# The fourth slot of a fused attention and mixture-of-experts kernel uses seven products

## The chip, the cores and the metric

The kernel runs on one core of one Trainium2 chip. A core has a matrix engine, TensorE (PE in the rows, with its weight loads as PEld), a vector engine, VectorE (DVE), a scalar engine, ScalarE (ACT), a general engine, GpSimd (POOL), and SyncE (SP), which here issues transfers. Each engine works through its own queue in order; they meet through semaphores. The metric is the time on the device in microseconds, lower is better.

## What is computed

An attention over a small memory feeds a mixture of experts. Eight batches of 576 tokens make 4608 tokens of 512 values (8 heads of 64):

```
a   = softmax(phi, over the 576 tokens)             # 32 memory slots per head
k_m = a^T k ;  v_m = a^T v                          # per batch and head
x   = softmax(q k_m^T / 8) v_m                      # 4608 x 512, all heads side by side
e   = argmax(x w_gate)                              # one of 8 experts per token
out = gate * sigmoid(x w_output_gate)[e] * (relu(x w1[e]) w2[e])   # 512 -> 1024 -> 512
```

Only the last line, the two layers of the experts, is touched by the change. The matmuls have to be nearly as exact as float32. Each operand is therefore kept as a high and a low part, and a product of two matrices is three matmuls (high by high, low by high, high by low: `PASS`).

## The kernel before

**Stages.** The attention runs batch pair by batch pair and writes the rows of x to a table in DRAM (`xs`). Routing counts the tokens of each expert and writes lists of rows. The experts' work is then done in *slots*: a slot is 576 tokens of one expert. Eight big slots are numbered 0 to 7. Slots 0 to 3 (`NPE`) are filled from the first half of the tokens, so they can start while the attention of the second half still runs; slots 4 to 7 (`NPL`) come from lists that the late routing writes (`route_late`). Slots 0 and 1 share their time with the rest of the attention, slot 2 begins when the late routing ends.

**One slot.** `nine` (L1382) does a slot. Its first layer gives 1024 hidden values per token, in matmuls of 288 columns (half a slot's tokens). It comes in two forms:
- `plain` (L1266, matmuls at L1278): 4 weight pieces x 2 x 2 halves of the tokens x 12 matmuls, used for the slots in `WHOLE`, 0 to 3;
- `seven` (L1285, matmuls at L1306 in `product`): both matrices are cut in two by two, and seven products of sums and differences replace eight products (Strassen's scheme in Winograd's form); each product is 4 x 6 matmuls. Its intermediate results are copied from PSUM into tiles `keep` (L1313) and added on DVE (L1317). Used for the slots in `SEVEN`, 4 to 7.

The second layer (L1409) takes 112 matmuls of 512 columns in either form. Its steps are numbered 16 to 35 after the 16 of the first layer; `finish_y` (L1227) scales its results and scatters them with an indirect transfer of POOL (L1237).

**Preparing the next slot.** This is done within the slot before, mostly in its second layer.
- `gather` (L463, transfers at L468): POOL fetches the 576 rows of the next slot, full rows of 576 floats, into tile `xg`. There is one such buffer.
- For a `plain` slot, `turn_x` (L1045) turns the rows on PE (16 of L1108 with 128 columns, 4 of L1113 with 64), ACT and DVE split the result into high and low parts (L1070, L1071).
- For a `seven` slot, `relay` (L474) copies `xg` in 16 transfers on SP (L484) from SBUF tile to SBUF tile into `xq`, so that DVE's transposes of 32 by 32 blocks (L1074) finish the turn. Then the differences of the parts (L1092), their high parts on ACT (L1086, L1095) and their low parts on DVE (L1097, L1100).
- Weights are loaded by SP (L522), split into high (ACT, L564) and low (DVE, L569). A `seven` slot also needs four sums of weight parts, `S1` to `S4` in `prep` (L526): S3, S1 and S4 on DVE (L538, L544, L546), S2 on POOL (L542).

**Layouts.** The memory is laid out anew as stages end. `settle` (L1481) follows slot 1. `reopen` (L1493) finishes the late routing, closes its pools, opens the pool `st` (which holds `xq`, `keep`, the sums and the parts of differences), and gives weights two more raw buffers, seven in all. `rebank` (L1502) cuts PSUM into two sets of four banks, and is called in a slot whose successor is a `seven` slot. `run` (L1508) walks over the slots and calls `reopen`; its `hook` is called after each step of a slot and issues the gathers, the copies of the relay (from steps `RELAY` = 5 and 8 of the slot before) and the steps of the routing. When a slot's successor is a `seven` slot, `nine` uses tables of its own for the order of the preparation (`TURN6`, `EXTRA6`, `SUMS6` after a `plain` slot, `TURN7`, `EXTRA7`, `SUMS7` after a `seven` slot).

Of the kernel before, what the change touches and what calls it, by code (L numbers as in the profile page):

```python
# [30 lines left out]
NPE, NPL, NSS = 4, 4, 28  # L31
# [31 lines left out]
EXTRA7 = (2, 6, 9, 12, 17, 19)  # L63
GATHER = {8: 2, 12: 2, 16: 1}
LAST = 1
OPEN = 3
WHOLE = tuple(range(NPE))
SEVEN = tuple(range(NPE, NPE + NPL))
PROD = ("P1", "P2", "P6", "P5", "P3", "P7", "P4")
SPLITS = {"P1": (0, 2), "P6": (2,), "P5": (0, 2)}  # L70
SUMS = {"P6": "S2", "P5": "S1", "P3": "S4", "P7": "S3"}
# [9 lines left out]
def attention_moe(tc, phiT, kv, qT, wgo, wall, out):  # L81
# [3 lines left out]
    with contextlib.ExitStack() as ctx:  # L85
# [343 lines left out]
        def force():  # L429
            clock[0] += 1  # L430
            (rou if rou.gens else late if late.gens else att).step()
# [22 lines left out]
        for s in range(NSLOT):  # L454
# [3 lines left out]
            slots.append({"s": s, "big": big, "q0": NCL * j if big else NCL * NPL + j - NPL, "idx": idx[nm],  # L458
                          "rows": 4 * S if s < NPE else NTOK, "nm": nm, "quart": s not in WHOLE, "seven": s in SEVEN,
                          "known": False, "listed": False})  # L460
# [13 lines left out]
        def relay(z, to=4):  # L474

            if not z["quart"]:
                return
            if "xq" not in z:
                z["xq"] = env["st"].tile([P, NCL, 4, P], F32, name="xq")
                z["a"] = 0  # L480
            for a in range(z["a"], to):
                for b in range(4):
                    m = 1 if not z["big"] else NCL if b < 2 else NCL - 1
                    nc.sync.dma_start(z["xq"][32 * a:32 * a + 32, 0:m, b],  # L484
                                      z["xg"][32 * b:32 * b + 32, 0:m, XQ * a:XQ * a + P])
                z["a"] = a + 1
# [109 lines left out]
        def gathers(i, must=0, n=999, to=2):  # L596

            while True:
                if drip.gens:
                    drip.step(999 if gat[0] <= must else n)  # L600
                    if drip.gens:
                        break
                    n = 0
                if gat[0] >= min(gat[1], i + to):
                    break
                z = order[gat[0]]
                if not z["listed"]:
                    if gat[0] >= must:
                        break
                    force()  # L610
                    continue
                if gat[0] >= must and n <= 0:
                    break
                drip.gens.append(gather(z))
                gat[0] += 1
# [589 lines left out]
        def grow(k):  # L1205
            nonlocal mo
            if k == 0:
                mo = ctx.enter_context(tc.tile_pool(name="mo", bufs=1, reuse_waits="tile"))
            for r, n in zip((ring, raw, xgs), GROW[k]):
                if n:  # L1210
                    p = ctx.enter_context(tc.tile_pool(
                        name=f"{r.name}{k + 1}", bufs=n, reuse_waits="tile"))
                    r.add(p, n)
# [267 lines left out]
        def settle():  # L1481

            att.finish()
            pso.close()
            pa.close()
            env["rl"] = prl.enter_context(tc.tile_pool(name="rl", bufs=1, side="right", reuse_waits="tile"))
            env["cap"] = raw.size
            grow(1)
            env["ps"] = prp.enter_context(tc.tile_pool(name="p1", bufs=7 - NPK, space=PSUM, reuse_waits="tile"))
# [3 lines left out]
        def reopen():  # L1493

            late.finish()
            prl.close()
            prt.close()
            env["st"] = ctx.enter_context(tc.tile_pool(name="st", bufs=1, side="right", reuse_waits="tile"))
            grow(2)
            env["cap"] = raw.size  # L1500
# [7 lines left out]
        def run(st):  # L1508

            lo, hi = st.lo, st.hi  # L1510
            while not order[lo]["known"]:
                force()
            st.fetch()
            if lo:
                gat[:] = lo, hi

            def hook(step, new):
                if step < 16 or not drip.gens:
                    gathers(i)
                if i + 1 < hi and order[i + 1]["seven"]:  # L1520
                    if step in RELAY and (gat[0] > i + 2 or gat[0] > i + 1 and not drip.gens):
                        relay(order[i + 1], 2 * RELAY.index(step) + 2)
                clock[0] += not att.gens
                att.step(HOOK[0])
                (rou if rou.gens else late).step(HOOK[1])

            for i in range(lo, hi):
                if i == OPEN:
                    reopen()
                gathers(i, i + 1, 0)  # L1530
                if i == lo:
                    for c in range(4):
                        turn_x(order[i], c)

                def nxt(c):
                    if i + 1 < hi:
                        gathers(i, i + 2)
                        turn_x(order[i + 1], c)

                if order[i]["big"]:  # L1540
                    nine(i, st, nxt, hook)
                else:
                    single(i, st, nxt)
                if "rl" not in env and (i == LAST or not att.gens):
                    settle()
# [5 lines left out]
        env["open"] = True  # L1551
        n = NPE + NPL
        run(stream)
        used = nc.values_load(slot[0:1, NSLOT:], min_val=0, max_val=NSS)  # L1554
        with tc.If(used > 0):
            run(Stream(n, n + 1))
            with tc.If(used > 1):
                run(Stream(n + 1, n + 4))
                with tc.If(used > 4):
                    run(Stream(n + 4, NSLOT))  # L1560
# [44 lines left out]
```

## Time and profile before

| | |
|---|---|
| median of 3 runs | 550.5 us (548.32 to 551.82) |
| profiled execution, its own time | 550.38 us |
| its span in the trace | 548.6 us |
| TensorE (PE) busy | 500.8 us, 91% |
| VectorE (DVE) busy | 362.8 us, 66% |
| ScalarE (ACT) busy | 273.0 us, 50% |
| GpSimd (POOL) busy | 175.0 us, 32% |
| mean over 16 DMA engines | 188 GB/s |

The page of the profile gives busy time per engine, and forty equal slices of the span with a digit for the busy tenths of each engine. The timeline lists instructions in order of their start, with like neighbours merged: start, length, engine, line, operation, what it writes and reads, count; brackets give the idle time before and what ended it. Matmuls overlap in the pipeline, so the length of one (0.29 us) is more than the step from one to the next (0.13 us); steps between starts are what counts.

### The profile page before, as it was taken

What the parts mean: (1) busy time and instruction counts of PE and PEld (TensorE: products, weight loads), DVE (VectorE), ACT (ScalarE), POOL (GpSimd) and SP (SyncE); (2) the same over time, 40 slices, a digit from 0 to 9 for tenths busy, and PEclk for the clock granted to TensorE, in tenths of its full rate; (3) what the DMA queues carried; (4) which work ended last, traced back from release to release, by engine and by line L of the source; (5) the groups of instructions that cost most, each with busy time, mean ns of one, the idle gap of its engine ahead of it and who ended that gap; (6) DMA issues with size and microseconds to landing.
All of it is one profiled execution on the core that took longest, in us unless ns stands there. A gap on an engine that the chain in (4) does not pass through costs nothing. (4 is left out here: it accounts for less than half of the span.)

```text
span 548.6 us, 10934 instructions
## 1 busy us (share of the span) xinstructions
PE 500.8 (91%) x4141; PEld 432.0 (79%) x4141; DVE 362.8 (66%) x802; ACT 273.0 (50%) x526; POOL 175.0 (32%) x202
## 2 busy tenths in 40 slices
PE   3688677759999999999999999999999999999993
PEld 2455445539987899889988998998899899889982
DVE  4387799766971678975424459578779867878500
ACT  4467474254643453243324325576485666648320
POOL 2334465554251233214022315512612350220021
PEclk9969998769999999999999999999999999999998
DMA  8999999976543575317332830891485179130011
GB/s 324 419 375 384 413 374 396 321 279 192 202 128 133 159 271 132 112 42 249 84 118 71 299 84 11 275 245 48 149 260 169 39 235 258 46 106 21 1 49 44
DMA packets 44414, 103.11 MB, mean 188 GB/s; under 512 B 9600, under 2 KB 18880, under 8 KB 43968
## 3 DMA queue, kind: packets, MB, share of 16 engines
q1 hardware_dynamic: 38464, 82.26, 45.3%
q0 software_dynamic: 5888, 20.06, 10.5%
q8 instruction: 34, 0.56, 0.4%
q14 instruction: 28, 0.23, 0.1%
HBM read 77.23 MB, written 20.35 MB: 178 GB/s over the span
## 5 line engine op out<-in xcount | busy, mean ns | idle before, releaser
L1409 PE MATMUL bps<-whl,hh 128*128 128x512 f32 x576 | 173.2, 393 | 0.0
L1409 PEld LDWEIGHTS bps<-whl,hh 128*128 128x128 f32 x576 | 107.5, 188 | 22.6
L569 DVE TENSOR_TENSOR whl<-w,whl 128x1024 fp32r<-128x1024 f32 x72 | 88.1, 1232 | 52.5 <-ACT whl L564 51.9
L1278 PE MATMUL bps<-xh,whl 128*128 128x288 f32 x512 | 105.1, 297 | 0.0
L1409 PE MATMUL bps<-whl,hl 128*128 128x512 f32 x224 | 87.3, 390 | 0.0
L1278 PEld LDWEIGHTS bps<-xh,whl 128*128 128x128 f32 x512 | 83.0, 188 | 1.3 <-issue 0.6
L564 ACT CAST whl<-w 128x1024 fp32r<-128x1024 f32 x72 | 74.6, 1049 | 3.2 <-PE bpc L1409 2.0
L1278 PE MATMUL bps<-xl,whl 128*128 128x288 f32 x256 | 75.5, 295 | 0.0
L1237 POOL DMA_INDIRECT out<-y,idx_oa x20 | 27.3, 1365 | 110.4 <-ACT y L1236 86.9
L1246 ACT ACTIVATE hh<-bps 128x288 fp32r<-128x288 f32 x64 | 26.4, 412 | 57.9 <-PE bps L1278 56.7
L1237 POOL DMA_INDIRECT out<-y,idx_ol x20 | 21.8, 1090 | 101.4 <-ACT y L1236 66.7
L1409 PEld LDWEIGHTS bps<-whl,hl 128*128 128x128 f32 x224 | 42.1, 188 | 8.2
L1278 PEld LDWEIGHTS bps<-xl,whl 128*128 128x128 f32 x256 | 48.3, 189 | 0.1
L1251 DVE SCALAR_TENSOR_TENSOR hl<-bps,hh 128x288 fp32r<-128x288 f32 x64 | 26.9, 421 | 31.7 <-ACT hh L1246 31.6
L1236 ACT ACTIVATE y<-bps,gx 128x512 f32<-128x512 f32 x28 | 19.3, 690 | 49.7 <-PE bps L1409 44.7
L1306 PE MATMUL bpc<-th,whl 128*128 128x288 f32 x192 | 39.7, 295 | 0.0
L1306 PE MATMUL bpc<-xh,whl 128*128 128x288 f32 x192 | 39.7, 295 | 0.0
L892 ACT COPY xo<-bpd 128x576 f32<-128x576 f32 x36 | 22.5, 639 | 25.2 <-PE bpd L890 17.6
L857 POOL TENSOR_TENSOR ea<-ea,mx 128x512 f32<-128x512 f32 (+1 forms) x20 | 19.2, 961 | 43.5 <-DVE mx L855 41.7
L1306 PEld LDWEIGHTS bpc<-xh,whl 128*128 128x128 f32 x192 | 31.3, 188 | 0.2
L1306 PEld LDWEIGHTS bpc<-th,whl 128*128 128x128 f32 x192 | 31.3, 188 | 0.0
L1246 ACT ACTIVATE hh<-keep 128x288 fp32r<-128x288 f32 x48 | 21.1, 446 | 18.8 <-DVE keep L1317 18.8
(263 smaller groups left out, 890.8 us busy)
## 6 DMA issues: line engine op xcount, KB each, us to landing
w<-wall SPq DMA_DIRECT2D x64, 512.0 KB, 5.1
kvt<-kv SPq DMA_DIRECT2D x32, 512.0 KB, 8.2
xs<-xo SPq DMA_DIRECT2D x16, 576.0 KB, 7.0
qt<-qT SPq DMA_DIRECT2D x16, 512.0 KB, 9.1
ph<-phiT SPq DMA_DIRECT2D x3, 1152.0 KB, 11.7
xq<-xg SPq DMA_DIRECT2D x32, 80.0 KB, 4.8
kv<-kv SPq DMA_DIRECT2D x4, 512.0 KB, 9.9
xq<-xg SPq DMA_DIRECT2D x32, 64.0 KB, 3.9
```

What stands on the lines that cost most here:

```text
L564: A.copy(hl[:, 0], w[:])
L569: V.tensor_tensor(hl[:, 1], w[:], hl[:, 0].bitcast(F32), ALU.subtract)
L857: G.tensor_tensor(eav, eav, mx[:, 0:n].unsqueeze(2).to_broadcast([P, n, M]), ALU.subtract)
L892: A.copy(xo[:, c % 2], px[:, :, 0:2 * XQ])
L1236: A.activation(y[0:n], py[0:n], AF.Copy, scale=z["g"][0:n, k:k + 1])
L1237: G.indirect_dma_start(out=out, out_offset=bass.IndirectOffsetOnAxis(ap=z["idx"][1][0:n, z["q0"] + k:z["q0"] + k + 1], axis=0), in_=y[0:n] ...
L1246: A.activation(h_[:, j, c:e], src, AF.Relu)
L1251: V.scalar_tensor_tensor(lo, src[:, s0 - c:s1 - c], 0.0, h_[:, j, s0:s1].bitcast(F32), ALU.max, ALU.subtract)
L1278: T.matmul(pb, w[:, b, o:o + P], x[a][:, cc, c * SL // 2:(c + 1) * SL // 2], start=(n == 0), stop=(n == 11))
L1306: T.matmul(pb, w[:, b, o:o + P], z[x][a][:, kc], start=(first and n == 0), stop=(n == 5), skip_group_check=not first)
L1409: T.matmul(py, a, w[:, b, DM * f:DM * f + DM], start=(u == 4 and f == 0 and n == 0), stop=(u == 7 and f == 1 and n == len(ps) - 1))
```

## The change

Three edits, in the tables at the head of the file and in `run`:
- `WHOLE` becomes slots 0 to 2 and `SEVEN` slots 3 to 7. Slot 3 takes the form `seven` with everything that belongs to it: weights in the other cut, `relay` in place of turns on PE, the four sums, the results kept in tiles.
- `OPEN` becomes `(2, 2)`: `reopen` is called from `hook` after step 2 of slot 2, instead of ahead of slot 3. Buffers of the pool `st` are needed then by slot 2's steps.
- With slot 3 a `seven` slot, slot 2 prepares by the tables `TURN6`, `EXTRA6`, `SUMS6` and calls `rebank`, as slot 3 does in the kernel before, and slot 3 prepares by `TURN7`, `EXTRA7`, `SUMS7`, as slots 4 to 6 do.

```diff
--- before.py
+++ after.py
@@ -63,9 +63,9 @@
 EXTRA7 = (2, 6, 9, 12, 17, 19)
 GATHER = {8: 2, 12: 2, 16: 1}
 LAST = 1
-OPEN = 3
-WHOLE = tuple(range(NPE))
-SEVEN = tuple(range(NPE, NPE + NPL))
+OPEN = (2, 2)
+WHOLE = tuple(range(NPE - 1))
+SEVEN = tuple(range(NPE - 1, NPE + NPL))
 PROD = ("P1", "P2", "P6", "P5", "P3", "P7", "P4")
 SPLITS = {"P1": (0, 2), "P6": (2,), "P5": (0, 2)}
 SUMS = {"P6": "S2", "P5": "S1", "P3": "S4", "P7": "S3"}
@@ -1515,6 +1515,8 @@
                 gat[:] = lo, hi
 
             def hook(step, new):
+                if (i, step) == OPEN:
+                    reopen()
                 if step < 16 or not drip.gens:
                     gathers(i)
                 if i + 1 < hi and order[i + 1]["seven"]:
@@ -1525,8 +1527,6 @@
                 (rou if rou.gens else late).step(HOOK[1])
 
             for i in range(lo, hi):
-                if i == OPEN:
-                    reopen()
                 gathers(i, i + 1, 0)
                 if i == lo:
                     for c in range(4):
```

On PE, in slot 2's second layer (the L1409 rows) and at its end; whl is a weight piece, xg the gathered rows, - is the kernel before, + the changed one:
```order
 L1409 MATMUL bps<-whl,hh 128x512
-L1108 MATMUL bps<-ident,xg 128x128 x4
-L1113 MATMUL bps<-ident,xg 128x64 x4
+L1306 MATMUL bpc<-xh,whl 128x288
+L1306 MATMUL bpc<-xl,whl 128x288
+L1306 MATMUL bpc<-xh,whl 128x288 x2
```
The turns are gone, here the first eight of twenty, and L1409 is followed by the first of the seven products. In the whole program L1108 and L1113 lose 16 and 4 instructions, L1278 loses 192 and L1306 gains 168.

On DVE, from the end of slot 2's first layer on; first the kernel before:
```order
L1251 SCALAR_TENSOR_TENSOR hh<-bps,hh 128x64
L569 TENSOR_TENSOR whl<-w,whl 128x1024
L1234 TENSOR_TENSOR y<-bps,y 64x512
L569 TENSOR_TENSOR whl<-w,whl 128x1024
L1071 TENSOR_TENSOR xl<-bps,xh 128x512
L1071 TENSOR_TENSOR xl<-bps,xh 128x4x64
L1071 TENSOR_TENSOR xl<-bps,xh 128x512 x3
```
and at the same place in the changed kernel (`s_3801` is the tile of S2):
```order
L1251 SCALAR_TENSOR_TENSOR hh<-bps,hh 128x64
L538 TENSOR_TENSOR w<-w 128x1024
L1074 STREAM_TRANSPOSE xg<-xq 128x576 x4
L1234 TENSOR_TENSOR y<-bps,y 64x512
L1092 TENSOR_TENSOR xq<-xg 128x576
L1092 TENSOR_TENSOR xq<-xg,xq 128x576
L1092 TENSOR_TENSOR xq<-xg 128x576
L1092 TENSOR_TENSOR xq<-xg,xq 128x576
L569 TENSOR_TENSOR whl<-s_3801,whl 128x1024
L1097 TENSOR_TENSOR xl<-xg,xh 128x576 x3
L544 TENSOR_TENSOR w<-s_3801,w 128x1024
L1100 TENSOR_TENSOR xl<-xq,xh 128x576
```
The low parts of turned rows give way to the transposes, differences and sums of a seven-product slot; the rows ahead of this place, the late routing's among them, stand as they did.

On POOL, from the gather for slot 3 (`idx_ga`) on; first the kernel before:
```order
L468 DMA xg<-xs,idx_ga 128x576 x4
L468 DMA xg<-xs,idx_ga 64x576
L1237 DMA out<-y,idx_oa 4608x512 x5
L468 DMA xg<-xs,idx_gl 128x576 x4
L468 DMA xg<-xs,idx_gl 64x576
L542 TENSOR_TENSOR s_4306<-w 128x512 x2
```
and the changed kernel:
```order
L468 DMA xg<-xs,idx_ga 128x576 x4
L468 DMA xg<-xs,idx_ga 64x576
L542 TENSOR_TENSOR s_3801<-w 128x512 x2
L1237 DMA out<-y,idx_oa 4608x512 x2
L468 DMA xg<-xs,idx_gl 128x576 x4
L468 DMA xg<-xs,idx_gl 64x576
```
The gather for slot 3 keeps its place, S2 for slot 3 comes behind it, and the gather for slot 4 (`idx_gl`) stands behind two of slot 2's outputs instead of five.

## Rows read from the trace of the kernel before

**Rows 1.** The page: TensorE's busy time, busy tenths and granted clock in 40 slices.
```profile
PE 500.8 (91%) x4141; PEld 432.0 (79%) x4141; DVE 362.8 (66%) x802; ACT 273.0 (50%) x526; POOL 175.0 (32%) x202
...
PE   3688677759999999999999999999999999999993
...
PEclk9969998769999999999999999999999999999998
```

**Rows 2.** Timeline of TensorE at the borders of slots and layers: start, length, instruction, count.
```profile
244.28 0.29 PE L1278 MATMUL bps<-xh,whl 128*128 128x288 f32 x1
...
269.71 1.55 PE L1409 MATMUL bps<-whl,hh 128*128 128x512 f32 x6
...
297.59 0.29 PE L1278 MATMUL bps<-xh,whl 128*128 128x288 f32 x1
...
348.44 0.29 PE L1306 MATMUL bpc<-xh,whl 128*128 128x288 f32 x1
```

**Rows 3.** Busy time by stretch, between the borders of layers, columns in its first line.
```profile
core 0: us, PE busy (x) PEld busy (x) DVE busy (x) ACT busy (x) POOL busy (x), PEclk, DMA share, GB/s
244.28:269.72 25.44, 25.44 (x194) 25.44 (x193) 13.63 (x31) 10.52 (x20) 7.23 (x6) 1.00 0.59 187
269.72:297.59 27.87, 27.87 (x134) 22.93 (x133) 7.74 (x11) 10.36 (x17) 3.94 (x4) 1.00 0.23 71
297.59:323.03 25.44, 25.44 (x194) 25.44 (x193) 13.24 (x28) 10.51 (x20) 7.24 (x6) 1.00 0.68 222
323.03:348.44 25.41, 25.41 (x115) 21.02 (x113) 18.18 (x24) 10.92 (x18) 14.44 (x8) 1.00 0.27 76
348.44:370.83 22.39, 22.39 (x169) 22.39 (x168) 17.25 (x39) 16.25 (x34) 5.68 (x5) 1.00 0.87 255
370.83:396.26 25.43, 25.43 (x114) 21.02 (x113) 21.43 (x28) 13.74 (x21) 11.04 (x9) 1.00 0.31 90
```

**Rows 4.** Timeline of TensorE in slot 2's second layer, at the first turns.
```profile
285.15 0.39 PE L1409 MATMUL bps<-whl,hl 128*128 128x512 f32 x1
285.38 0.39 PE L1409 MATMUL bps<-whl,hh 128*128 128x512 f32 x1
285.61 0.60 PE L1108 MATMUL bps<-ident,xg 128*128 128x128 f32 x4
...
286.53 0.50 PE L1409 MATMUL bps<-whl,hh 128*128 128x512 f32 x1
```

**Rows 5.** Timeline of POOL, SP and DVE in slot 3: preparation of slot 4.
```profile
300.13 1.52 POOL L468 DMA_INDIRECT xg<-xs,idx_gl  x1 [0.30 <-issue]
...
313.75 10.98 SPq L484 DMA_DIRECT2D xq<-xg  x16
...
326.51 2.76 DVE L1074 STREAM_TRANSPOSE xg<-xq 128x576 f32<-128x576 f32 x4 [1.19 <-DMA xq<-xg]
...
333.68 2.09 DVE L1097 TENSOR_TENSOR xl<-xg,xh 128x576 fp32r<-128x576 f32 x3
...
339.50 1.22 DVE L546 TENSOR_TENSOR w<-w,s 128x1024 f32<-128x1024 f32 x1
...
336.55 6.19 POOL L1237 DMA_INDIRECT out<-y,idx_oa  x1 [4.44 <-ACT y L1236]
```

**Rows 6.** Timeline of POOL, SP and DVE at the start of slot 2.
```profile
247.24 1.10 POOL L468 DMA_INDIRECT xg<-xs,idx_ga  x1 [0.31 <-issue]
...
252.57 1.68 POOL L468 DMA_INDIRECT xg<-xs,idx_ga  x1 [0.30 <-issue]
...
253.47 0.33 SPq L522 DMA_DIRECT2D w<-wall  x1
...
244.74 0.21 DVE L264 SCALAR_TENSOR_TENSOR idx_ol<-iv,i 128x48 int32<-128x48 f32 x1
```

**Rows 7.** Timeline at the end: TensorE's last matmul and the last output.
```profile
539.52 0.39 PE L1409 MATMUL bpc<-whl,hh 128*128 128x512 f32 x1
...
541.33 0.98 POOL L1237 DMA_INDIRECT out<-y,idx_ol  x1 [4.87 <-ACT y L1236]
```

## The prediction

> **What bounds the kernel now.** I read the page first: TensorE (PE) is busy for 91% of the span, and in its forty slices PE is at 9 from the tenth slice to the last but one, with the granted clock at 9 or more there, which is the 2.4 GHz level [rows 1]. So the question is not which engine is busiest, but whether PE ever waits in the stretch that the change touches. I then cut the span at the borders of the slots, read from the timeline of PE (a slot's first layer begins with L1278 or L1306, its second with L1409) [rows 2], and asked for the busy time of each engine between those borders [rows 3]. There PE is busy for the whole of every stretch: 25.44 of 25.44, 27.87 of 27.87 us and so on, at clock 1.00. No engine has to become faster for this stretch to become shorter; instructions have to leave PE.
>
> The same table gives the price of each layer directly, as lengths:
> - first layer without products saved (slots 2 and 3): 25.44 us each;
> - first layer of seven products (slots 4 and 5): 22.39 and 22.40 us;
> - second layer with the next slot's twenty PE turns in it (slot 2): 27.87 us;
> - second layer before a seven-product slot, so without turns: 25.41 us (slot 3) and 25.43 us (slot 4).
>
> **The change part by part.**
> *Fewer matmuls.* Slot 3's first layer has 4 x 2 x 2 x 12 = 192 matmuls now and will have 7 x 4 x 6 = 168. By the lengths that is 25.44 - 22.39 = 3.05 us (24 matmuls at 25.44/192 = 0.1325 us are 3.18 us; the seven-product layer runs at 22.39/168 = 0.1333 us). Slot 3's second layer goes from 25.41 to 25.43 us, since it now prepares slot 4 from a seven-product slot: +0.02. Together -3.03 us.
>
> *Turns leave PE.* Sixteen L1108 and four L1113 instructions go from slot 2's second layer. By the lengths, 27.87 - 25.41 = 2.46 us. The timeline agrees for the first eight of them: from the matmul at 285.38 to the next one at 286.53 are 1.15 us, of which one matmul's own step is 0.23 (285.15 to 285.38), so 0.92 us for eight [rows 4]; the remainder, 1.54 us, leaves 0.51 us for each of the three groups of four that follow.
>
> The Trainium skill's page "TensorE: Matmul & The Clock Gate", section "Back-to-back issue gap", gives N/2.4 + 2.5 ns for a warm matmul of N columns: 122.5 ns for 288 columns and about 56 ns for a turn of 128. By it the 24 matmuls would be 2.94 us and the twenty turns an estimated 1.1 us, 4.1 us in all and 546.3 us for the kernel. This case's lengths are larger for both (132.5 ns a matmul, 2.46 us for the turns), and the sum goes by the lengths.
>
> *What takes their place, and what hides it.* The preparation that slot 3 now makes for slot 4 will be made once more, in slot 2 for slot 3: gather into xg, sixteen copies from SBUF tile to SBUF tile on SP (L484), then S3, four transposes, four differences, the low parts and the sums on VectorE (DVE), S2 on GpSimd (POOL). The trace shows this very sequence in slot 3 [rows 5]: gather issued from 300.13, copies from 313.75 for 10.98 us, transposes at 326.51, the operands of the first product finished at 333.68 + 2.09 = 335.77, the last sum of weights at 339.50 + 1.22 = 340.72. Slot 4 begins at 348.44 [rows 2]. So the first operands have 12.7 us of slack and the last item of the list 7.7 us, and PE does not wait. I take 7.7 as the slack, the smaller.
>
> In slot 2 it starts at nearly the same phase: the gather for slot 3 is already there, issued from 247.24, 2.96 us into the slot (slot 4's: 300.13, 2.54 us into slot 3), its last piece issued at 252.57 + 1.68 [rows 5, 6]. Weights have two more buffers from the end of the third step on (249.05 by 25.44/16 = 1.59 us a step), so the loads ahead of the copies on SP come no later than now (the one at 253.47 is the next of them). Engines have room: DVE is busy 7.74 us of slot 2's second layer and would go to about the 18.18 of slot 3's; slot 3 itself would go from 13.24 to about 17.25 of 22.4, and to 21.4 of 25.4, the load which slots 4 and 5 carry without a wait of PE [rows 3]. I charge nothing for it: nothing as long as the lateness stays below 7.7 us, and each microsecond beyond is a microsecond of PE.
>
> *The late layout entered earlier.* Line for line its only cost is that the first writers into the new buffers must wait for the last reader of the old ones. Routing's last result, idx_ol, is written at 244.74, 0.5 us into slot 2 [rows 6], and the entry is at 249.05, so I charge zero. With no routing left to hurry, nothing is pulled forward on PE's queue either.
>
> *Slot 4's gather* is queued on POOL behind two outputs in slot 2's second layer instead of five. One such output took 6.19 us in slot 3 (at 336.55, among DVE's work on SBUF operands) where others take about 1 us [rows 5]. If that repeats, the gather still goes out in the order in which slot 5's did, and the slot behind it ran at its usual 22.39 us [rows 3]. Zero again.
>
> *The sum.* -3.03 - 2.46 = -5.49 us. PE stays at 9 tenths and full clock from slot 3 to the last slice but one [rows 1]; after its last matmul at 539.52 one output goes out at 541.33 [rows 7]. Everything behind slot 3 therefore moves forward whole, and the tail of some 9 us stays. The profiled execution took 550.38 us, so 544.9; the median of the three runs shown is 550.5, 0.1 above it, so **545.0 us**.
>
> **The rivals.**
> 1. *Only part arrives.* The new preparation in slot 2 is 8 to 12 us later than the same work in slot 3, by the DMA queues (slot 2's first layer has the copies and two earlier loads added to what rows 3 show, 0.59 of the DMA engines busy against 0.68 in slot 3). PE then waits once, at slot 3's first product, by up to 4 us: 546 to 549, middle 547.5. Against it: the phases of rows 5 and 6 differ by 0.4 us, not 8.
> 2. *The turns are worth less on PE alone.* Part of the 2.46 us could be some other wait of slot 2's second layer that stays. If half of it stays, 1.23 us, the time is 546.1. Against it: PE shows no idle time in this stretch, and the first eight turns are seen step for step [rows 3, 4]. The Trainium skill's figure above ("TensorE: Matmul & The Clock Gate") points to this side.
> 3. *Slower: the entry holds SP.* SP works in order. If a buffer of the late layout lies where a reader finishes late, its load, the sixteen copies behind it and all later weights stand. Up to 7.7 us cost nothing, 13.2 eat the whole gain, 18.7 make it slower by 1%. If the entry were held to the end of slot 2's first layer (269.71, 20.7 us after the entry), PE would lose 20.7 - 7.7 = 13.0 us: 544.9 + 13.0 = 558. Against it: the last routing write stands at 244.74, before the entry.
> 4. *It does not do what it says* can be left out: the order shows the 24 matmuls and 20 turns gone.
> 5. *More than the sum*, by 2 us or more, below 543: I see no mechanism but the spread of the runs (548.32 to 551.82).
>
> **How the numbers follow.** The forecast has 0.80, rival 1 has 0.10, rival 2 has 0.04, rival 3 has 0.03, rival 5 has 0.03. About 1% is what a measurement of this kernel can tell from no change; here that is 5.5 us, and the forecast of 5.49 stands on the bound itself. Its 0.80 therefore divides evenly: faster 0.40 + 0.03 = 0.43, same 0.40 + 0.10 + 0.04 = 0.54, slower 0.03. The forecast's own range is 545.0 with the runs' half spread of 1.75: 543.2 to 546.8. To hold 8 in 10 the range takes in rival 2 and most of rival 1 and leaves the ends of both sides out: 543.0 to 548.0.
>
> **What would show each step.** Slot 2's second layer should be 25.4 us long with no L1108 in it, slot 3's first 22.4 us of L1306, and from slot 4 on every border should stand 5.5 us earlier, with PE busy for the whole of each stretch. DVE's transposes for slot 3 should start about 28 to 29 us into slot 2 and its last sum of weights end some 8 us before slot 3. The prediction is wrong if PE has idle time at slot 3's first product (rival 1 or 3: then look at what the copies on SP or the transposes waited for), if slot 2's second layer is longer than 25.5 us with no idle time (rival 2), or if a later slot lengthens, which would mean that one more slot of dense DVE work is not free.

## The result, and the profile after

| | before | after |
|---|---|---|
| median of the runs, us | 551.16 (548.32 to 552.31, 4 runs) | 543.76 (542.56 to 544.02, 4 runs) |
| ratio | | 0.9869, 95% interval 0.9827 to 0.9911 |
| profiled execution, us | 550.38 | 544.02 |
| its span, us | 548.6 | 542.3 |
| first matmul of slot 2, us | 244.28 | 244.82 |
| last matmul of the kernel, us | 539.52 | 534.57 |
| stretch between these two, us | 295.24 | 289.75 |
| from the last matmul to the end of the span, us | 9.08 | 7.73 |

The changed kernel is faster by 1.3% (0.9 to 1.7 by the interval). The time of 543.8 lies in the range (543.0 to 548.0), 1.2 us below the forecast of 545.0. The gain is 7.4 us in the medians where the sum gave 5.49, and the class that came, faster by over 1%, had 0.43 against 0.54 for the same.

The page of the changed kernel, in the lines that answer to [rows 1]: TensorE's busy time and instructions, its busy tenths and its granted clock in 40 slices.

```profile
PE 497.3 (92%) x4097; PEld 428.5 (79%) x4097; DVE 380.5 (70%) x830; ACT 282.3 (52%) x543; POOL 178.3 (33%) x204
...
PE   3778786849999999999999999999999999999994
...
PEclk9969899778999999999999999999999999999998
```

44 matmul instructions are gone (24 products' matmuls and 20 turns), DVE has 17.7 us more to do, and PE still stands at 9 tenths and full clock from the tenth slice to the last but one. So PE still sets the time there, and its borders can be compared as before. Busy time of each engine between the borders of the layers of slots 2 (two rows), 3 (two rows) and 4 (its first layer), the answer to [rows 3]:

```profile
core 0: us, PE busy (x) PEld busy (x) DVE busy (x) ACT busy (x) POOL busy (x), PEclk, DMA share, GB/s
244.82:270.25 25.43, 25.43 (x193) 25.43 (x192) 13.64 (x31) 10.52 (x20) 7.22 (x6) 1.00 0.68 217
270.25:295.67 25.42, 25.42 (x115) 21.04 (x114) 18.19 (x24) 10.92 (x18) 13.46 (x8) 1.00 0.27 77
295.67:318.06 22.39, 22.39 (x170) 22.39 (x168) 17.25 (x39) 16.25 (x34) 5.40 (x5) 1.00 0.87 259
318.06:343.49 25.43, 25.43 (x114) 21.03 (x113) 21.43 (x28) 13.74 (x21) 11.03 (x9) 1.00 0.31 86
343.49:365.88 22.39, 22.39 (x169) 22.39 (x168) 17.25 (x39) 16.25 (x34) 3.82 (x4) 1.00 0.90 263
```

Slot 2's second layer went from 27.87 to 25.42 us and slot 3's first from 25.44 to 22.39, with PE busy for the whole of each. The preparation behind it, timeline of SP, DVE and POOL in slot 2 (the answer to [rows 5], where the same work stands in slot 3):

```profile
262.29 10.44 SPq L484 DMA_DIRECT2D xq<-xg  x16
...
274.41 2.76 DVE L1074 STREAM_TRANSPOSE xg<-xq 128x576 f32<-128x576 f32 x4 [1.86 <-DMA xq<-xg]
...
281.58 2.09 DVE L1097 TENSOR_TENSOR xl<-xg,xh 128x576 fp32r<-128x576 f32 x3
...
287.40 1.22 DVE L546 TENSOR_TENSOR w<-w,s 128x1024 f32<-128x1024 f32 x1
...
284.79 5.87 POOL L1237 DMA_INDIRECT out<-y,idx_oa  x1 [4.75 <-ACT y L1236]
290.96 1.04 POOL L468 DMA_INDIRECT xg<-xs,idx_gl  x1 [0.30 <-issue]
```

The copies begin 17.5 us into the slot (262.29 - 244.82), 1.3 us later than in slot 3 of the kernel before: the gather's last piece is issued by 254.79, and SP waits 7.8 us for the gather to land before the first copy. The transposes begin 29.6 us into the slot. The first operands are done at 283.67, 12.0 us ahead of slot 3's start at 295.67, and the last sum of weights at 288.62, 7.05 us ahead. The slow output came again (5.87 us, 6.19 before), and the gather for slot 4 behind it still goes out 4.7 us ahead of slot 3.

The stretch is shorter by 295.24 - 289.75 = 5.49 us: the sum to the hundredth. The other part of the gain lies behind the last matmul, where 9.08 us became 7.73. The end of the changed kernel, the answer to [rows 7]:

```profile
534.57 0.39 PE L1409 MATMUL bpc<-whl,hh 128*128 128x512 f32 x1
...
536.38 0.98 POOL L1237 DMA_INDIRECT out<-y,idx_ol  x1 [4.86 <-ACT y L1236]
```

From the last matmul to the last output's issue are 1.81 us, as before (539.52 to 541.33). What became shorter comes after that.

### The profile page after: what moved, and what is told of

Same layout as the page of the kernel before. It is cut to its first block, busy times and chain, and to the rows that moved or that the text cites. A ratio compares the mean times of both kernels' runs of the same rounds, so it can differ in the third digit from the quotient of the medians.

```text
span 542.3 us, 10918 instructions
## 1 busy us (share of the span) xinstructions
PE 497.3 (92%) x4097; PEld 428.5 (79%) x4097; DVE 380.5 (70%) x830; ACT 282.3 (52%) x543; POOL 178.3 (33%) x204
## 5 line engine op out<-in xcount | busy, mean ns | idle before, releaser
L1409 PE MATMUL bps<-whl,hh 128*128 128x512 f32 x560 | 167.2, 392 | 0.0
L1409 PEld LDWEIGHTS bps<-whl,hh 128*128 128x128 f32 x560 | 104.6, 188 | 21.9
L1409 PE MATMUL bps<-whl,hl 128*128 128x512 f32 x216 | 84.2, 390 | 0.0
L1278 PE MATMUL bps<-xh,whl 128*128 128x288 f32 x384 | 79.2, 297 | 0.0
L1278 PEld LDWEIGHTS bps<-xh,whl 128*128 128x128 f32 x384 | 62.2, 188 | 1.2 <-issue 0.6
L1278 PE MATMUL bps<-xl,whl 128*128 128x288 f32 x192 | 56.6, 295 | 0.1
L1306 PE MATMUL bpc<-th,whl 128*128 128x288 f32 x240 | 49.6, 295 | 0.0
L1306 PE MATMUL bpc<-xh,whl 128*128 128x288 f32 x240 | 49.6, 295 | 0.0
L1409 PEld LDWEIGHTS bps<-whl,hl 128*128 128x128 f32 x216 | 40.6, 188 | 8.1
L1306 PEld LDWEIGHTS bpc<-xh,whl 128*128 128x128 f32 x240 | 39.1, 188 | 0.2
L1306 PEld LDWEIGHTS bpc<-th,whl 128*128 128x128 f32 x240 | 39.1, 188 | 0.0
L1278 PEld LDWEIGHTS bps<-xl,whl 128*128 128x128 f32 x192 | 36.1, 188 | 0.4 <-DVE xl L1071 0.3
L1306 PE MATMUL bpc<-xl,whl 128*128 128x288 f32 x120 | 35.4, 295 | 0.0
L1306 PE MATMUL bpc<-tl,whl 128*128 128x288 f32 x120 | 35.4, 295 | 0.0
```

The lines of the kernel that those rows point to most:

```text
L1278: T.matmul(pb, w[:, b, o:o + P], x[a][:, cc, c * SL // 2:(c + 1) * SL // 2], start=(n == 0), stop=(n == 11))
L1306: T.matmul(pb, w[:, b, o:o + P], z[x][a][:, kc], start=(first and n == 0), stop=(n == 5), skip_group_check=not first)
L1409: T.matmul(py, a, w[:, b, DM * f:DM * f + DM], start=(u == 4 and f == 0 and n == 0), stop=(u == 7 and f == 1 and n == len(ps) - 1))
```

## The experiments

Each run is read in two parts of its profile: the stretch from slot 2's first matmul to the kernel's last, and the end behind it. The first is where the edit acts. Where slot 2 begins (243.6 to 248.1 us) differs from profile to profile without regard to the edit, so it is left out. The last two columns compare the two parts with the medians: (stretch - 295.24) + (end - 9.08), and the median less that of the kernel before in the same session.

| run | stretch, us | end, us | POOL instructions | sum of the two parts | median less before |
|---|---|---|---|---|---|
| before | 295.24 | 9.08 | 409 | | |
| the changed kernel | 289.75 | 7.73 | 414 | -6.84 | -7.4 |
| the same, again (r1) | 289.75 | 7.70 | 414 | -6.87 | -6.7 |
| e1, entry alone | 295.24 | 8.88 | 409 | -0.20 | -0.2 |
| e2, turns put back | 292.25 | 7.65 | 414 | -4.42 | -4.3 |
| e3, an eighth product | 292.95 | 7.94 | 414 | -3.43 | -3.4 |
| e4, turns gone alone | 292.77 | 8.62 | 409 | -2.93 | -1.7 |
| e5, copies issued later | 289.75 | 9.65 | 412 | -4.92 | -4.1 |
| e6, gather 8 us late | 289.75 | 7.62 | 428 | -6.95 | -6.2 |
| e7, gather 16 us late | 298.07 | 7.53 | 442 | +1.28 | +1.0 |
| e8, before with 5 on POOL | 294.93 | 7.11 | 414 | -2.28 | -1.8 |
| e9, before with 3 on POOL | 294.93 | 9.38 | 412 | -0.01 | +0.4 |

POOL instructions are those of its queue up to and with its last branch, the small ones counted too. The parts come from one profile of each kernel, the medians from all its runs.

**The changed kernel again.**

> The changed kernel once more. Theory 1 (only PE's own time went): between slot 2's first matmul and the last matmul of the program the profile is 5.5 us shorter than before (539.52 - 244.28 = 295.24 us before, 289.75 now), and whatever the total shows beyond 5.5 us lies ahead of slot 2 or behind the last matmul; ratio about 0.990. Theory 2 (something else became faster too, 1 to 2 us): that stretch itself is shortened by 6.5 us or more, or the head or tail is shorter in every run; ratio about 0.987.

Measured: 544.8 us (541.67 to 545.37, 6 runs) against 551.53, ratio 0.9864 (0.9835 to 0.9893). The gain repeats with 6.7 us, and so do stretch and end to 0.03 us. A shorter end in two profiles of the same kernel speaks against chance.

**The entry alone (e1).** Only the place of the late layout's entry is that of the changed kernel; the slots keep their kinds of before.

```diff
-WHOLE = tuple(range(NPE - 1))
-SEVEN = tuple(range(NPE - 1, NPE + NPL))
+WHOLE = tuple(range(NPE))
+SEVEN = tuple(range(NPE, NPE + NPL))
```

> The late layout is entered in slot 2 (after its third step), and slot 3 keeps its eight products and its turns on PE. Theory 1: the same time as before, ratio 1.000 (0.998 to 1.002), slot 2 53.3 us and slot 3 50.85 us long. Theory 2, if the two earlier weight buffers are what gave the rest: 1 to 2 us faster than before. The rival of the prediction in which the entry holds SP: slower by 5 us or more, with PE idle in slot 2.

Measured: 551.36 us against 551.53, ratio 0.9992 (0.9967 to 1.0017), and a stretch of 295.24 us, equal to the kernel before's to the hundredth. The entry costs nothing and gives nothing. Rival 3 is refuted: no wait at the entry reaches PE here, and none does in the changed kernel, where the copies stand behind the entry in SP's queue.

**The turns put back (e2).** In the changed kernel, twenty turns of the identity go into a PSUM bank that nobody reads, at the places where slot 3's turns stood.

```diff
+            if z["s"] == 3:
+                pt = bank([512], "ps")
+                for k in range(4):
+                    T.transpose(pt[:, k * P:(k + 1) * P], ident[:], ident[:])
+                if c == 0:
...
+                        T.transpose(pt[:, e], ident[0:64], ident[0:64, 0:64])
```

> The changed kernel with sixteen turns of 128 columns and four of 64 put back on PE in slot 2's second layer, at the places where they were, on the identity matrix, with nothing that reads them. Theory 1: slot 2's second layer is 27.9 us instead of 25.4, the kernel 2.5 us slower than the changed one. The rival (half of the 2.46 us was another wait): 1.2 us slower, second layer 26.6 us.

Measured: 547.28 us, 2.5 above the changed kernel in the same session; the stretch grew by 2.50 us. Timeline of PE in this run, at the begin and the end of slot 2's second layer:

```profile
273.54 1.77 PE L1417 MATMUL bps<-whl,hh 128*128 128x512 f32 x7
...
301.45 0.29 PE L1314 MATMUL bpc<-xh,whl 128*128 128x288 f32 x1
```

301.45 - 273.54 = 27.91 us, where the changed kernel has 25.42 and the kernel before had 27.87. The twenty turns are worth their 2.46 us on PE and nothing else was in that length: rival 2 is refuted. The Trainium skill's page "TensorE: Matmul & The Clock Gate", section "Back-to-back issue gap", calls the formula that gave an estimated 1.1 us the gap of an isolated matmul; for a stream with weight loads it states some 81 ns per matmul of 128 columns, by which the twenty would be an estimated 1.6 us. This trace agrees with neither: the 2.50 us decide.

**An eighth product (e3).** Slot 3's first layer computes one of its seven products twice, 24 matmuls more.

```diff
             for f in range(4):
+                if i == 3:
+                    product("P4", "T4", bank([SL // 2], "ps"), f, first=True)
                 product("P4", "T4", pbs[f], f)
```

> The changed kernel in which slot 3 alone computes its last product twice, the extra one into a bank that nothing reads: 24 matmuls of 288 columns more. Theory 1: slot 3's first layer 22.39 + 24 x 0.1333 = 25.6 us, the kernel 3.2 us slower than the changed one. If matmuls were not what bounds this layer but DVE or ACT: less than 1 us slower.

Measured: 548.15 us, 3.4 above the changed kernel; the stretch grew by 3.20 us, which is 24 x 0.1333, the step that the prediction read from the layer of seven products.

**The turns gone, the products not (e4).** Slot 3 gets its rows by copies and transposes on DVE, but its first layer has the 192 matmuls of before and takes the weight pieces of before, so that its products join rows and weights of two different orders.

```diff
-SEVEN = tuple(range(NPE - 1, NPE + NPL))
+SEVEN = tuple(range(NPE, NPE + NPL))
...
-... :, u + 8 * (z["quart"] and u < 4)])
+... :, u + 8 * (z["quart"] and u < 4 and z["s"] != 3)])
...
-                if i + 1 < hi and order[i + 1]["seven"]:
+                if i + 1 < hi and order[i + 1]["quart"]:
```

> The kernel before with one part of the change: slot 3's rows are turned by the copies between SBUF tiles and DVE's transposes, with the entry in slot 2, but slot 3 keeps its eight products with the weights in the old cut (its features are then in another order than its weights, so its outputs are not the reference's). Theory 1: slot 2 is 2.5 us shorter than before (50.85 instead of 53.31), the kernel 2.5 us faster, ratio 0.9955. If the copies are in each other's way or late: less, and PE idle at the border of slots 2 and 3.

Measured: 549.53 us against 551.19, ratio 0.9969 (0.9948 to 0.9991). The stretch is 2.47 us shorter, the turns' 2.46; slot 2's second layer is 25.41 us long (273.55 to 298.96). The median gained 1.7, less than the 2.9 of the two parts, but the interval (0.5 to 2.9 us) reaches that far.

**The copies issued later in the program (e5).** In slot 2 the sixteen copies are no longer issued a few per step, but all at the step where the transposes are.

```diff
-                if i + 1 < hi and order[i + 1]["seven"]:
+                if i != 2 and i + 1 < hi and order[i + 1]["seven"]:
```

> The changed kernel in which the sixteen copies for slot 3 are issued in slot 2's second layer (its third step, about 28.3 us into slot 2) instead of in the first layer (about 15.4 us into it): some 12.8 us later. If the slack is the 7.7 us that the prediction took (up to the last sum of weights), PE waits 5 us in slot 3 and the kernel is 5 us slower than the changed one. If the slack is the 12.7 us of the first product's operands, and everything later is needed later, PE waits 0 to 1 us.

This run missed its aim. SP's queue in slot 2 of this run:

```profile
255.99 0.33 SPq L522 DMA_DIRECT2D w<-wall  x1
263.64 10.44 SPq L484 DMA_DIRECT2D xq<-xg  x16
291.13 5.33 SPq L522 DMA_DIRECT2D w<-wall  x2
```

Slot 2 begins at 246.80 here, so the copies stand 16.8 us into it, not later than the changed kernel's 17.5. Between the load at 255.99 and the copies SP waits 7.2 us for the gather to land. The copies go by the data, and a later place in the program is no later time for a queue that would wait anyway. The stretch is the changed kernel's, 289.75. And yet the run is slower than that kernel: 547.11 us against 551.19 for before, a gain of 4.1 instead of 6.7. Its end is 9.65 us instead of 7.7. That was the hint that the end depends on something that has no part in PE's work; by the count of instructions, this kernel has two fewer on POOL.

**The gather late (e6, e7).** In the changed kernel, POOL fills an unused tile 14 (e6) or 28 times (e7) ahead of the gather for slot 3. This makes the preparation late by data, with nothing else moved.

```diff
             z["xg"] = xgs.tile()
+            if z["s"] == 3:
+                for _ in range(14):
+                    G.memset(idle[:], 0.0)
```

> The changed kernel with 14 memsets of 128x512 on POOL ahead of the gather for slot 3, so that gather, copies and all that follows them in slot 2 come later; 0.3 us for a memset of 64x256 in the trace of before gives an estimate of 8 us for the fourteen. If the slack is the 7.7 us that the prediction took (here some 7 us, as the copies start 1.3 us later in their slot than slot 4's do), PE waits about 1 us. If only the operands of the first product count (12 us of slack here), PE does not wait and the stretch from slot 2 to the last matmul is 289.75 us, as in the changed kernel.

> The same with 28 memsets, an estimate of 17 us. With 7 us of slack PE waits 10 us; with 12 us it waits 5 us, at slot 3's first product, and the stretch from slot 2 to the last matmul becomes 295 us, as long as before the change: this is the lateness at which the change gains nothing on PE.

e6: 544.73 us (2 runs) against 550.92. POOL is held for 8.16 us, but the copies, which had waited for the gather to land, begin only 3.1 us later: 20.55 us into the slot instead of 17.5, and the first operands are done 42.6 us into it instead of 38.85. PE waits for nothing and the stretch is 289.75: a lateness of 3 to 4 us is free.

e7: 551.95 us against 550.92, ratio 1.0015 (0.9984 to 1.0046): the whole gain is eaten. Slot 2 begins at 244.70. Timeline of POOL, SP, DVE, ACT and PE in this run, from the fills to slot 4 (lines are 4 further down than in the changed kernel, so L1240 is the output y, L1310 the seven products, L550 the last sum of weights):

```profile
247.35 16.30 POOL L468 MEMSET idle<- 128x512 f32 x28
...
274.03 10.43 SPq L488 DMA_DIRECT2D xq<-xg  x16
...
293.30 2.09 DVE L1101 TENSOR_TENSOR xl<-xg,xh 128x576 fp32r<-128x576 f32 x3
...
299.12 1.22 DVE L550 TENSOR_TENSOR w<-w,s 128x1024 f32<-128x1024 f32 x1
...
300.43 1.05 ACT L568 CAST whl<-w 128x1024 fp32r<-128x1024 f32 x1 [2.23 <-DVE w L550]
301.38 0.68 ACT L1240 ACTIVATE y<-bps,gx 128x512 f32<-128x512 f32 x1
...
302.11 0.40 PE L1310 MATMUL bps<-xh,whl 128*128 128x288 f32 x1 [0.81 <-ACT y L1240]
...
302.68 1.04 POOL L472 DMA_INDIRECT xg<-xs,idx_gl  x1 [0.30 <-issue]
...
332.41 2.76 DVE L1078 STREAM_TRANSPOSE xg<-xq 128x576 f32<-128x576 f32 x4 [7.50 <-DMA xq<-xg]
...
352.49 0.40 PE L1310 MATMUL bpc<-xh,whl 128*128 128x288 f32 x1 [2.35 <-ACT y L1240]
```

The copies are 11.9 us later in the slot than the changed kernel's (29.3 against 17.5). The first operands come at 295.39, just ahead of slot 3's first matmul at 295.55; the last sum of weights ends at 300.34, 4.8 us behind it. ACT's cast of weights waits 2.23 us for it, the output y of slot 2 stands behind that cast in ACT's queue, and PE's bank comes free only with y. PE's waits in this run, in slot 3 first and then in slot 4 (what PE waited for; us in total, times, longest):

```profile
PE bpc L1310 <- ACT keep L1317: 1.7, 3, 1.3
PE bps L1310 <- ACT y L1240: 0.8, 1, 0.8
PE bpc L1310 <- DVE hh L1255: 0.3, 1, 0.3
...
PE bpc L1310 <- ACT y L1240: 2.3, 1, 2.3
```

PE does not wait for slot 3's first product, whose operands were just in time; the first of its five waits ends at 302.11, 6.6 us into the slot.

Slot 3's first layer is 26.60 us long instead of 22.39, and slot 4's 26.50: 4.2 and 4.1 us, 8.3 in all. The second payment has its own chain. Slot 2's outputs on POOL wait for ACT, whose casts of the late operands come first, and the gather for slot 4 is behind these outputs, the last of which takes 5.87 us again: it goes out at 302.68, 7.1 us into slot 3, where the changed kernel has it 4.7 us ahead of slot 3. Then slot 4's copies and transposes are late in turn (DVE sat idle for 7.50 us for the copies), and PE waits 2.35 us in slot 4. Not all of the 4.1 us is waiting, though. Busy time and granted clock of the two first layers, and PE's timeline behind the wait in slot 4:

```profile
core 0: us, PE busy (x) PEld busy (x) DVE busy (x) ACT busy (x) POOL busy (x), PEclk, DMA share, GB/s
295.55:322.15 26.60, 23.77 (x169) 22.54 (x168) 24.15 (x47) 19.02 (x39) 13.18 (x8) 1.00 0.61 199
347.60:374.10 26.50, 24.15 (x170) 23.92 (x169) 22.74 (x45) 17.20 (x35) 9.93 (x8) 0.94 0.88 263
...
353.99 0.44 PE L1310 MATMUL bps<-xl,whl 128*128 128x288 f32 x1
354.23 0.68 PE L1310 MATMUL bps<-xh,whl 128*128 128x288 f32 x2
...
357.43 0.29 PE L1310 MATMUL bps<-xl,whl 128*128 128x288 f32 x1
```

In slot 3 the granted clock stays at 1.00 through all five waits. In slot 4 it falls soon after the one long wait: it is 0.50, the 1.2 GHz level, from 354 to 356 us, and is back at 1.00 by 358. The fifteen matmuls from 353.99 to 357.43 take 3.44 us, where they take 2.00 at 0.1333 us each. So an estimated 1.4 of the 4.1 us is the lower clock, and 2.7 the wait. Slot 5 and the later slots show no wait of PE.

**Two tiny instructions on POOL (e8, e9).** The kernel before, with 5 (e8) or 3 (e9) fills of one column of an unused tile on POOL ahead of the gather for slot 3. PE's instructions are those of before.

```diff
             z["xg"] = xgs.tile()
+            if z["s"] == 3:
+                for _ in range(5):
+                    G.memset(idle[:], 0.0)
```

> The kernel before with five more tiny memsets on POOL in slot 2, so that POOL has as many instructions as in the changed kernel; PE's work is untouched. Theory 3 (the 1.3 us behind the last matmul hang on how many instructions stand ahead of the end in POOL's queue, not on the seven products): the stretch from slot 2 to the last matmul is 295.24 us as before, the rest of the span behind it about 7.7 us instead of 9.1, the kernel 1.3 us faster than before, ratio 0.9976. If the tail became shorter for another reason of the change: 9.1 us and the same time as before.

> The same with three more memsets on POOL, as many instructions as in the run with the copies issued late in the text, whose span behind the last matmul was 9.65 us. Theory 3: 9.65 us here too, the kernel 0.5 us slower than before and 1.9 us slower than with five. Otherwise: no difference from before or from five.

Measured: e8 549.1 us, ratio 0.9963 (0.9936 to 0.9990); e9 551.31 us, ratio 1.0001 (0.9974 to 1.0028). Two fills of one column are all that tells them apart, and the medians differ by 2.2 us, the ends by 2.27 (7.11 and 9.38). The stretch is 294.93 us in both, 0.31 less than was expected, so of the 2.28 us that e8's profile gains over the kernel before the end has 1.97. The last matmul, first of e8, whose span is 547.4 us, then of e9 with 547.9:

```profile
540.29 0.39 PE L1413 MATMUL bpc<-whl,hh 128*128 128x512 f32 x1
...
538.52 0.39 PE L1413 MATMUL bpc<-whl,hh 128*128 128x512 f32 x1
```

Here is the place of it, in the view of the source lines at the end (queue, instruction and count: durations in ns, first and last start in us): POOL's four semaphore instructions behind its last branch, and the first of its drains, of e8:

```profile
L1559 POOLq EVENT_SEMAPHORE  x4: 17/43/43, 545.2 to 545.4; - x4
...
L1605 POOLq DRAIN  x3: 45/107/733, 545.9 to 547.2; - x3
```

and of e9:

```profile
L1559 POOLq EVENT_SEMAPHORE  x4: 17/43/43, 543.5 to 545.8; - x4
...
L1605 POOLq DRAIN  x3: 45/107/733, 546.3 to 547.6; - x3
```

The four take 0.2 us in e8 and 2.3 in e9. In e5, also with 412 instructions, they take 2.3 (541.4 to 543.7). The kernel before, with 409, has its pause a few instructions later:

```profile
L1555 POOLq EVENT_SEMAPHORE  x4: 17/43/43, 544.8 to 545.0; - x4
...
L1601 SPq EVENT_SEMAPHORE  x14: 17/28/28, 545.4 to 548.5; - x14
L1601 POOLq DRAIN  x3: 45/107/875, 546.9 to 548.3; - x3
```

Here the four take 0.2 us, but POOL's drain comes 1.5 us after SP's first instruction of the line. In the changed kernel it comes 0.1 us after it:

```profile
L1555 POOLq EVENT_SEMAPHORE  x4: 17/43/43, 539.6 to 539.8; - x4
...
L1601 SPq EVENT_SEMAPHORE  x14: 17/28/28, 540.2 to 542.2; - x14
L1601 POOLq DRAIN  x3: 45/107/733, 540.3 to 542.0; - x3
```

So POOL pauses at a place that goes by the number of instructions, and the traces give that place exactly: behind the 414th instruction of POOL's queue. With 409 instructions up to the last branch (before, e1, e4) this is 5 instructions behind the branch, and the pause is 1.4 us; with 412 (e5, e9) it is 2 behind it, and the pause is 2.1 us. With 414 (the changed kernel, r1, e2, e3, e8) it is the branch itself, behind which POOL stands still for 2.6 to 3.0 us in every run whatever its count, and no second pause is seen. In e6, where the 414th stands earlier, in slot 7, POOL goes on after 0.2 us. That the end goes by the number of POOL's instructions is shown by e8 against e9.

What POOL does in the pause is only argued. In all five traces that have it, one packet of 8192 bytes of the instruction queue q14 ends 1.0 to 1.1 us before POOL goes on, which would fit the loading of its next instructions. But such packets pass in the traces without the pause too, and their number (28 before, 29 after, 27 in e8, 28 in e9) doesn't order the runs.

## Why the prediction was right, and where it was off

- **What bounds the kernel.** Right. PE had no wait between slot 2 and the end before, and has none after.
- **Fewer matmuls, 3.03 us.** Right. Slot 3's first layer is 22.39 us long; put back in e3, 24 matmuls cost 3.20.
- **Turns, 2.46 us.** Right: 27.87 to 25.42, 2.47 alone in e4, 2.50 put back in e2. The 1.1 us that the prediction set beside this took the formula of an isolated matmul and 128 columns for all twenty, where four turns have 64; the sum does not use it. Together with the products the stretch lost 5.49 us, the sum as it stood. Reading a change's price as the difference of two layers of the same trace was better than any price of one instruction.
- **The preparation, at nothing.** Right for this kernel: 7.05 us of slack for the last sum and 12.0 for the first operands, where 7.7 and 12.7 were read from slot 3. The gather went out early, as read, but the copies had to wait for it to land and began 1.3 us later in the slot than slot 4's had, so the phases are not as near as the 0.4 us that the prediction took from the gathers' issue. DVE's busy times came as written (18.19, 17.25 and 21.43 us in the three layers). Rival 1 fell with it: 1.3 us late, not 8 to 12.
- **"Each microsecond beyond is a microsecond of PE."** Too mild. By it, e7's copies, 11.9 us late, would cost 11.9 - 7.05 = 4.8 us; slot 3 paid 4.2, which the rule has about right, and slot 4 paid another 4.1. The gain of 5.49 was already gone at this lateness, where the prediction put that point at 13.2. That the last sum of weights sets the slack is right, since e7's first wait goes back to it; at which lateness the waiting begins, between 3.8 (e6) and 11.8 us (e7) for that sum, no run shows. Two things were missing: a late slot hands its lateness on to the next through ACT's and POOL's queues (an estimated 2.7 us), and a wait can be followed by a lower granted clock (an estimated 1.4 us). The wait does not come at slot 3's first product either, as rivals 1 and 3 had it, but behind ACT's queue some 6 us later.
- **The entry and slot 4's gather, at nothing.** Right: e1 shows the first, and the slow output of 5.87 us came again without a cost to PE.
- **"The tail of some 9 us stays."** This is the step that failed. It became 1.35 us shorter, and this is why the gain in the profiles is 6.84 and in the medians 6.7 to 7.4 instead of 5.49. The prediction took the end as fixed since no line of it is in the change. But the change takes POOL from 409 to 414 instructions, and in e8 five tiny ones alone shorten the end by 1.97 us. Rival 5, more than the sum, was given 0.03 with "no mechanism but the spread of the runs"; 543.8 us is only 0.8 above its 543. There was a mechanism, though nothing in the trace of before alone would have given its sign: three more instructions (e9) leave the end at 9.38, five more bring it to 7.11.
- **The chances.** The forecast of 5.49 us stood on the bound of 1% (5.5), so its chance was cut in two halves, and the rivals that were worse then tipped the balance to the same. The 1.35 us of the end put the kernel over the bound: the sum alone would have stood on it, and on which side was luck.

## What to carry to other kernels

Where one engine is busy for the whole of a stretch, take the price of an edit as the difference in length of two stretches of the same trace that differ only by it: here it was right to the hundredth. When charging a move at nothing, read the slack of every item it hands on, and follow a lateness through the in-order queues into the slot behind, since it may be paid twice, and look at the granted clock behind each long wait. And hold the end of a program apart from its body: two tiny instructions on an engine that is far off the path moved it by more than 2 us, nearly as much as twenty turns cost.

## What the runs showed that was not expected

- The time behind the last matmul goes by the number of POOL's instructions: 8.6 to 9.1 us at 409 (three profiles), 9.4 to 9.65 at 412 (two), 7.1 to 7.9 at 414 (five), 7.5 and 7.6 at 442 and 428. Of the difference between e8 (7.1) and the changed kernel (7.7) at the same 414, 0.4 us is a wait behind POOL's first drain, 0.47 us in the changed kernel and 0.05 in e8.
- In e8 and e9, whose instructions on PE are those of before, the stretch is 294.93 instead of 295.24 us; their layers of seven products take 22.31 instead of 22.39 us. No run tells why.
- One output among DVE's work on operands of SBUF took 6.19 us on POOL before and 5.87 after, at the same place of a slot, where others take about 1. What holds it was not tried.
